# Attention, dense layer and routed experts on one core: three scheduling numbers moved

## The chip, the cores and the metric

The kernel runs on one core of one Trainium2 chip. The core's engines are TensorE (PE in the profile, with its weight loads as PEld), VectorE (DVE), ScalarE (ACT), GpSimd (POOL) and SyncE (SP), each working through its own instructions in order, and DMA queues that are fed by SP and POOL. The metric is the device time of one execution in microseconds; lower is better. Times are medians of several runs.

## What is computed

Three stages follow each other on 3072 tokens of width 384. First a gated linear attention over 4 sequences of 768 tokens with 8 heads of 48; then a dense layer 384 to 2048 to 384 with a leaky relu; then a layer of 8 experts to which the tokens are given greedily by their gate logits, 384 tokens to each.

```
for t in range(S):                                   # attention
    state = f[:, :, t, :, None] * state + np.einsum('bhd,bhe->bhde', k[:, :, t], v[:, :, t])
    y[:, :, t] = np.einsum('bhd,bhde->bhe', q[:, :, t], state)
...
h = x @ w_in                                         # dense layer
x = maximum(0.01 * h, h) @ w_out
...
logits = x @ w_gate                                  # routing: best pair first
for idx in argsort(-logits.flatten()):
    tok, e = idx // E, idx % E
    if assigned[tok] >= 0 or counts[e] >= N // E: continue
    assigned[tok] = e; counts[e] += 1
for e in range(E):                                   # experts
    h = maximum(x[assigned == e] @ w1[e], 0.0)
    out[assigned == e] = h @ w2[e]
```

## The kernel before

**Tiles.** The tokens are cut into 24 tiles of 128, taken chunk by chunk: tile n is chunk n // 4 of sequence n % 4. Precision is kept by splitting a number into a high and a low half of 16 bits, so a product takes three matmuls. The wide matmul of the kernel has 128 rows of weights and 384 columns; there are 3456 of them, in the dense layer (tiles `hp` and `xp`) and in the experts (`hp` from `x2T`, and `yp`).

**Attention of a tile.** `s0` sums logarithms of the forget gate (PSUM tile `P`), `s1` makes decayed queries and keys `qs` and `ks`, `s3` the scores `A`, `s2` transposes the keys on PE into PSUM (`kT`) and copies them on ACT to SBUF (`kp`), and `s4` makes the output `y` and the update `U` of the state, for which it reads `kp`. `attention()` walks over the tiles and gives one part, then yields a number of nanoseconds (`pace()`, 2300 once the dense layer runs), then the next part: `kT` in the third part of a tile and `y` and `U` one pace behind it. Tiles below FT = 8 are written out in another order at the start.

**Beside it.** The wide matmuls of the dense layer are the main stream. `Driver` advances a clock by the time of each wide matmul and puts the next part of a side generator into the program when its yield has run out; so a yield of 2300.0 stands for some 14 wide matmuls. The tile framework then sets the final order of each engine by its own priorities, unless `tc.keep_in_program_order` holds an instruction where it was written. Weights of the experts are loaded (`xw_s`), split on ACT (`xw_h`) and DVE (`xw_l`) and stored beside the dense layer. `gate_columns()` turns the rows of the second dense weight by a DMA transpose on SP's queue (`turned`) and multiplies them with the gate (`pg`, 12 small matmuls, 16 times); GP is the yield between the issue of a transpose and the matmuls of the one before it.

**Routing.** `route()` runs 7 rounds beside the last part of the dense layer and the first experts. A round looks for a threshold in 7 steps. Each step compares on DVE (`ge`), counts on PE (`c4`, six small matmuls), picks on DVE (`cm`, `cd`), sums on PE (`cnt`), compares on DVE (`ok`) and sums on PE (`tot`). At its end `slots_of` makes sums over tokens on PE (`ps`), and DVE works from them (`totc`, `inc`, `s1`) to the state of the next round, whose first step needs `ge` of some 29 DVE instructions later. The yield ahead of the first `c4` of a round is GAP[4] = 3400. For each finished round `token_list()` makes the list of tokens: DVE rows `ohs`, `h12`, `rh`, then PE `pi`, DVE, PE `pj`, DVE `idx` and `row`.

**Experts.** `fetch_weights` loads the weights of expert r (`w1e`, `w2e`) with POOL's queue; `fetch_tokens` gathers its tokens on POOL's queue (`xg`, three gathers) and turns them on SP's queue (`x2T<-xg`, three transposes). POOL also makes four of the eight `hl` halves of experts 1 to 5 and issues the scattered stores (`out`). All of them stand in one row on POOL. `w1e` of expert 7 waits until the three transposes of expert 6 have landed.

Every engine instruction goes through one helper, so the profile gives line 85 for all; rows are told apart by the names of their tiles. The profile drops trailing digits of names, so `c4` is `c`, `s1` is `s`, `x48` and `x2` are `x`.

Of the kernel before, what the change touches and what calls it, by code (L numbers as in the profile page):

```python
# [92 lines left out]
def body(tc, qk, v, f_logit, w_in, w_out, w_gate, w1, w2, out):  # L93
# [8 lines left out]
    E = w_gate.shape[1]  # L102
    NT = B * S // 128
# [7 lines left out]
    LEAD, PACE0, W0, FT, PB = 3, 1300.0, 1000.0, 8, 3  # L111

    with ExitStack() as ctx:
# [16 lines left out]
        def mm(o, l, r, start, stop):  # L130
            return PE.matmul(o, l, r, start=start, stop=stop, skip_group_check=True)
# [192 lines left out]
        XW = 768  # L324
        xw_s, xw_o = [], []
        assert SW1 == SW2
        PX, GP = 21, 3000.0

        turned_at = []
        fed, big = [], [0]  # L330
# [382 lines left out]
        def small(shape, name, dt=F32, bufs=2):  # L713
            return rw.tile(shape, dt, name=name, bufs=bufs)
# [6 lines left out]
        def route():  # L721
# [6 lines left out]
            for rnd in range(E - 1):  # L728
# [15 lines left out]
                oh = small([128, E, NT], "oh", BF16)  # L744
                DVE.tensor_tensor(oh, wdx, am[:, None, :].to_broadcast([128, E, NT]), op=OP.is_equal)
                DVE.scalar_tensor_tensor(v, d0, 1.0, un, op0=OP.add, op1=OP.mult)
                for l, (sh, w, T) in enumerate(LEVELS):
                    G = 128 // T
                    ge = small([128, NT * 32], "ge", BF16)[:, :NT * T].rearrange("p (a t g) -> p a t g", t=T, g=G)
                    va = v.rearrange("p (a g) -> p a g", g=G)[:, :, None, :].to_broadcast([128, NT // G, T, G])  # L750
                    DVE.tensor_tensor(ge, va, R["thr"][l], op=OP.is_ge)
                    if l == 0:
                        di = small([128, len(LEVELS) - 1, NT], "di", I32)
                        DVE.tensor_tensor(di, key[:, None, :].to_broadcast([128, len(LEVELS) - 1, NT]), R["sh"], op=OP.logical_shift_right)
                        DVE.tensor_tensor(di, di, R["mk"], op=OP.bitwise_and)
                        dg = small([128, len(LEVELS) - 1, NT], "dg", BF16)
                        DVE.scalar_tensor_tensor(dg, di, 1.0, R["unit"], op0=OP.add, op1=OP.mult)
                    yield GAP[0] if l else GAP[4]
                    c4 = bank([128, E, G], "c4")
                    for a in range(NT // G):  # L760
                        mm(c4, ge[:, a], oh[:, :, a * G:(a + 1) * G], a == 0, a == NT // G - 1)
                    wt = T.bit_length() - 1
                    cm = small([128, E * 8], "cm", F16)[:, :E * G].rearrange("p (e g) -> p e g", g=G)
                    DVE.tensor_tensor(cm, c4, R[f"diag{wt}"], op=OP.mult)
                    cd = R[f"cd{l % 2}"]
                    with nc.allow_low_precision("one count and zeros"):
                        DVE.tensor_reduce(cd[:, :E], cm, axis=AX.X, op=OP.add)
                    yield GAP[1]
                    cnt = bank([128, 32], "cnt")
                    mm(cnt[:, :T], cd, R[f"sel{wt}"], True, True)  # L770
                    ok = small([128, 32], "ok", BF16)
                    DVE.tensor_scalar(ok[:, :T], cnt[:, :T], kcap, None, op0=OP.is_ge)
                    yield GAP[2]
                    tot = bank([128, 32], "tot")
                    mm(tot[:, :T], R["bits"], ok[:, :T], True, True)
                    J = small([128, 1], "J")
                    scr = small([128, 32], "scr")
                    DVE.tensor_scalar(scr[:, :T], tot[:, :T], STEP[l], None, op0=OP.min, op1=OP.add, accum_out=J)
                    if l + 1 < len(LEVELS):
                        vp = v  # L780
                        v = small([128, NT], "v", BF16, 3)
                        DVE.scalar_tensor_tensor(v, vp, J, dg[:, l, :], op0=OP.subtract, op1=OP.add)
# [69 lines left out]
        GAP = (1700.0, 700.0, 550.0, 2000.0, 3400.0)  # L852
# [20 lines left out]
        def token_list(r, s):  # L873

            si = small([128, NT], "si", I32)
            DVE.tensor_scalar(si, s, -1.0, None, op0=OP.add)
            lo = small([128, NT], "lo", I32)
            DVE.tensor_scalar(lo, si, 31, None, op0=OP.bitwise_and)
            hi = small([128, NT], "hi", I32)
            DVE.tensor_scalar(hi, si, 5, None, op0=OP.arith_shift_right)  # L880
            lob = small([128, NT], "lob", BF16)
            DVE.tensor_scalar(lob, lo, 1.0, None, op0=OP.add)
            hib = small([128, NT], "hib", BF16)
            DVE.tensor_copy(hib, hi)
            yield 2500.0 if r else 600.0

            G = 4
            one = rw.tile([128, NT // G, 32, G], BF16, name="ohs", bufs=1)
            for h in range(2):
                x = slice(NT // G // 2 * h, NT // G // 2 * (h + 1))  # L890
                lg4 = lob.rearrange("p (a g) -> p a g", g=G)[:, x, None, :].to_broadcast([128, NT // G // 2, 32, G])
                DVE.tensor_tensor(one[:, x], lg4, R["thr5"][:, x], op=OP.is_equal)
                yield 300.0
            h12 = small([128, 12, NT], "h12", BF16)
            DVE.tensor_tensor(h12, hib[:, None, :].to_broadcast([128, 12, NT]), R["i12"], op=OP.is_equal)
            rh = small([128, 2, 12, NT], "rh", BF16)
            DVE.tensor_tensor(rh[:, 0], h12, R["jn"], op=OP.mult)
            DVE.tensor_scalar(rh[:, 1], h12, pcol, None, op0=OP.mult)
            yield 1500.0 if r == E - 2 else 1800.0
            pi = bank([128, 24, G], "pi")  # L900
            for a in range(NT // G):
                mm(pi, one[:, a], rh[:, :, :, a * G:(a + 1) * G].rearrange("p v h g -> p (v h) g"),
                   a == 0, a == NT // G - 1)
            pm = small([128, 24, G], "pm", F16)
            DVE.tensor_tensor(pm, pi, R["d15"][:, None, :].to_broadcast([128, 24, G]), op=OP.mult)
            pd = small([128, 24], "pd", F16)
            with nc.allow_low_precision("one whole number and zeros"):
                DVE.tensor_reduce(pd, pm, axis=AX.X, op=OP.add)
            yield 1200.0
            pj = bank([128, 6, 4], "pj")  # L910
            mm(pj, R["join"], pd, True, True)
            pq = small([128, 6, 4], "pq")
            DVE.tensor_tensor(pq, pj, R["quarter"][:, None, :].to_broadcast([128, 6, 4]), op=OP.mult)
            ti = small([128, 2, 3], "ti")
            DVE.tensor_reduce(ti.rearrange("p a b -> p (a b)"), pq, axis=AX.X, op=OP.add)
            idx = rw.tile([128, 3], I32, name="idx", bufs=E)
            DVE.scalar_tensor_tensor(idx, ti[:, 0, :], 128.0, ti[:, 1, :], op0=OP.mult, op1=OP.add)

            row = rw.tile([128, 3], I32, name="row", bufs=E)
            if r:  # L920
                DVE.tensor_scalar(row, idx, 1.0, None, op0=OP.add)
            else:
                f = small([128, 3], "f3")
                DVE.tensor_scalar(f, idx, 1.0, None, op0=OP.add)
                DVE.scalar_tensor_tensor(row, f, float(NT * 128 - 128), f, op0=OP.is_le, op1=OP.mult)
                DVE.tensor_scalar(R["place"], R["i384"], s[:, NT - 1:NT], None, op0=OP.is_equal)
            LISTS["x", r] = row, idx
# [147 lines left out]
        n = 0  # L1075
# [8 lines left out]
        def pace():  # L1084
            return 2300.0 if started else 1300.0
# [69 lines left out]
        def attention():  # L1155

            def finish(n):
                if (n < 0) or ("x", n) in complete:
                    return
                g, m = where[n]  # L1160
                if m == 0:
                    while g > 1 + done[0]:
                        yield 1000.0
                go("x", n)

            for n in range(NT):
                if ("x", n) in complete:
                    loads_after(n)
                    continue
                go("f", n + 1)  # L1170
                go("f", n + 2)
                go("p", n)
                go("a", n)
                yield pace()
                yield from finish(n - 1)
                go("p", n + 1)
                go("v", n)
                go("v", n + 1)
                yield pace()
                go("k", n)  # L1180
                yield pace()
                go("y", n)
                loads_after(n)
                yield pace()
            yield from finish(NT - 1)
# [156 lines left out]
```

## Time and profile before

| what | value |
|---|---|
| time, median of 3 runs | 754.88 us (753.85 to 755.87) |
| profiled execution, its own time | 762.14 us |
| its span, first to last instruction | 760.4 us |
| PE busy | 724.9 us, 95% of the span |
| DVE, ACT, POOL busy | 546.9, 338.8, 90.6 us |
| granted TensorE clock, mean | 0.990 |

PE is the engine to look at; the others are idle for a good part of the span. The profiled execution took 7.3 us more than the median. Busy time of PE is a union of matmuls that overlap: two wide matmuls in a row start 0.16 us apart, and each one's record lasts 0.33 us. The table of waits lists for each engine what it stood idle for, by the tile of the instruction that waited and the instruction that released it. The timeline gives start, length, engine, operation and tiles, with the idle time ahead and its releaser in brackets.

### The profile page before, as it was taken

The page shows a single profiled execution, that of the slowest core. Times are in us where ns is not written, and L with a number is a line of the kernel's source. Part 1 is how long each engine was busy: PE and PEld are TensorE (multiplying, and loading weights), DVE is VectorE, ACT ScalarE, POOL GpSimd, SP SyncE. Part 2 cuts the span into 40 slices and gives each one's busy share as a digit, 9 for nine tenths or more (in the row PEclk, how much of TensorE's full clock was granted, in tenths as well). Part 3 has the DMA queues.
Part 4 walks back from the last instruction along what each step waited for, and adds up shares of the span by engine and source line. Part 5 has one row for each costly group of instructions (what it writes and reads, how often), then busy time and mean ns, then how long its engine had stood idle before and what let it go on. Part 6 is the DMA issues. An engine that isn't in the chain of part 4 may idle for free.

```text
span 760.4 us, 15364 instructions
## 1 busy us (share of the span) xinstructions
PE 724.9 (95%) x5871; PEld 473.4 (62%) x5871; DVE 546.9 (72%) x1611; ACT 338.8 (45%) x704; POOL 90.6 (12%) x120
## 2 busy tenths in 40 slices
PE   8997999989999999999999999999999899999995
PEld 6774666667676677676666566555555455566563
DVE  7999999979857877876954758677686675863220
ACT  7677655557746755654744542000123123222220
POOL 3000000000000000000000001010234434534311
PEclk9998999999999999999999999999999999999998
DMA  9998555889896899998999200040475657664700
GB/s 235 216 235 218 141 155 137 205 242 256 225 290 172 263 273 220 250 278 215 238 254 247 94 2 13 22 187 22 155 223 164 189 151 180 215 173 142 252 32 32
DMA packets 116443, 137.08 MB, mean 180 GB/s; under 512 B 67729, under 2 KB 99474, under 8 KB 114322
## 3 DMA queue, kind: packets, MB, share of 16 engines
q1 hardware_dynamic: 110994, 101.50, 51.4%
q0 software_dynamic: 5376, 34.61, 13.4%
q8 instruction: 46, 0.75, 0.4%
q14 instruction: 27, 0.22, 0.1%
HBM read 86.52 MB, written 34.60 MB: 159 GB/s over the span
## 4 chain that ended last, share of the span: by engine, by line
PE 45%; DVE 25%; DMA 10%; issue 9%; ACT 4%; SPq 3%; POOL 2%; another core or an unknown queue 0%; POOLq 0%; ACTq 0%; DVEq 0%
PE xp L85 16%; PE hp L85 15%; PE yp L85 5%; DVE g L85 4%; DVE gl L85 3%; DMA xw_s<-in_moe_w 3%; PE y L85 3%; SPq L85 3%; DVE woutu L85 2%; DMA fT<-in_f_logit 2%; PE c L85 1%; ACT g L85 1%; PE A L85 1%; DVE am L85 1%; DVE xw_l L85 1%
## 5 line engine op out<-in xcount | busy, mean ns | idle before, releaser
L85 PE MATMUL hp<-xT,winh 128*128 128x384 f16 x768 | 192.2, 330 | 7.1 <-ACT winh L85 3.6
L85 PE MATMUL xp<-wo,gh 128*128 128x384 f16 x768 | 191.0, 326 | 1.0 <-ACT wo L85 1.0
L85 PE MATMUL hp<-xT,winl 128*128 128x384 f16 x384 | 126.6, 330 | 0.7 <-DVE winl L85 0.7
L85 PE MATMUL xp<-wo,gl 128*128 128x384 f16 x384 | 124.8, 325 | 0.0
L85 PEld LDWEIGHTS <-gh 128*128 128x128 f16 x912 | 83.6, 97 | 43.7 <-issue 1.2
L85 PEld LDWEIGHTS <-winh 128*128 128x128 f16 x768 | 73.6, 99 | 51.0 <-issue 6.1
L85 PE MATMUL hp<-x2T,w1e 128*128 128x384 f16 x576 | 99.0, 325 | 0.9 <-DVE x2T L85 0.5
L85 PE MATMUL yp<-w2e,hh 128*128 128x384 f16 x384 | 94.5, 325 | 0.0
L85 DVE SCALAR_TENSOR_TENSOR g<-hp,g 128x384 f32<-128x384 f32 x128 | 70.2, 554 | 26.1 <-ACT g L85 25.5
L85 ACT ACTIVATE g<-hp 128x384 f32<-128x384 f32 x148 | 70.0, 484 | 37.7 <-PE hp L85 25.8
L85 PEld LDWEIGHTS <-w1e 128*128 128x128 f16 x576 | 52.4, 97 | 33.8 <-issue 1.6
L85 ACT ACTIVATE xw_h<-xw_s 128x768 f16<-128x768 f32 x64 | 53.2, 840 | 30.4 <-DMA xw_s<-in_moe_w 24.5
L85 ACT ACTIVATE gh<-g 128x768 f16<-128x768 f32 x64 | 53.9, 842 | 28.5 <-DVE g L85 28.4
L85 PEld LDWEIGHTS <-gl 128*128 128x128 f16 x528 | 48.6, 97 | 28.8 <-issue 1.0
L85 DVE TENSOR_TENSOR gl<-g,gh 128x768 f16<-128x768 f32 x64 | 60.9, 952 | 2.3 <-ACT gh L85 2.3
L85 PE MATMUL yp<-w2e,hl 128*128 128x384 f16 x192 | 62.5, 325 | 0.0
L85 DVE SCALAR_TENSOR_TENSOR xw_l<-xw_s,xw_h 128x768 f16<-128x768 f32 x64 | 60.2, 952 | 1.2 <-ACT xw_h L85 1.1
L85 ACT ACTIVATE hh<-hp 128x384 f16<-128x384 f32 x64 | 31.3, 490 | 62.6 <-PE hp L85 50.2
L85 POOL IOTA jp<- 128x128 f32 x2 | 0.5, 237 | 454.7 <-PE hp L85 454.7
L85 DVE SCALAR_TENSOR_TENSOR hl<-hp,hh 128x384 f16<-128x384 f32 x44 | 24.3, 555 | 41.7 <-ACT hh L85 40.5
L85 PEld LDWEIGHTS <-winl 128*128 128x128 f16 x384 | 37.8, 99 | 24.9 <-DVE winl L85 2.0
L85 ACT ACTIVATE x<-yp 128x384 f32<-128x384 f32 x24 | 11.8, 490 | 92.2 <-PE yp L85 85.1
(262 smaller groups left out, 1116.5 us busy)
## 6 DMA issues: line engine op xcount, KB each, us to landing
xw_s<-in_moe_w SPq DMA_DIRECT2D x64, 384.0 KB, 4.1
qkT<-in_qk SPq DMA_DIRECT2D x48, 192.0 KB, 5.1
wout_s<-in_moe_w_out SPq DMA_DIRECT2D x16, 384.0 KB, 3.2
w1d<-xw_h SPq DMA_DIRECT2D x32, 192.0 KB, 3.3
w1d<-xw_l SPq DMA_DIRECT2D x32, 192.0 KB, 4.4
w2d<-xw_h SPq DMA_DIRECT2D x32, 192.0 KB, 3.7
w2d<-xw_l SPq DMA_DIRECT2D x32, 192.0 KB, 4.1
fT<-in_f_logit SPq DMA_DIRECT2D x24, 192.0 KB, 3.2
```

The costliest lines, as they stand in the source:

```text
L85: i = f(*args, **kwargs)
```

## The change

Three things are moved; nothing is added or removed. For tiles from FT on, `kT` is recorded one pace earlier, so two paces ahead of `y` and `U`. GP goes from 3000 to 4200. In rounds 1 to 3 the yield ahead of the first `c4` goes from 3400 to 5300 and these six matmuls are held in program order; and for the lists of rounds 1 and 2 the yield ahead of `pi` goes from 1800 to 3300.

```
-        PX, GP = 21, 3000.0
+        PX, GP = 21, 4200.0
...
-                    yield GAP[0] if l else GAP[4]
+                    yield GAP[0] if l else 5300.0 if 0 < rnd < 4 else GAP[4]
                     c4 = bank([128, E, G], "c4")
                     for a in range(NT // G):
-                        mm(c4, ge[:, a], oh[:, :, a * G:(a + 1) * G], a == 0, a == NT // G - 1)
+                        i = mm(c4, ge[:, a], oh[:, :, a * G:(a + 1) * G], a == 0, a == NT // G - 1)
+                        if l == 0 and 0 < rnd < 4:
+                            tc.keep_in_program_order(i)
...
-            yield 1500.0 if r == E - 2 else 1800.0
+            yield 1500.0 if r == E - 2 else 3300.0 if 0 < r < 3 else 1800.0
             pi = bank([128, 24, G], "pi")
...
                 go("v", n + 1)
+                if n >= FT:
+                    go("k", n)
                 yield pace()
-                go("k", n)
+                if n < FT:
+                    go("k", n)
                 yield pace()
                 go("y", n)
```

ACT, attention tile 13, the stretch ahead of its `ys<-y` (rows with - stand before, with + after):

```order
 L85 ACTIVATE xw_h<-xw_s 128x768
+L85 ACTIVATE kp<-kT 128x512
 L85 ACTIVATE gh<-g_2403 128x768
-L85 ACTIVATE xw_h<-xw_s 128x768
-L85 ACTIVATE kp<-kT 128x512
-L85 ACTIVATE xw_h<-xw_s 128x768
+L85 ACTIVATE xw_h<-xw_s 128x768 x2
 L85 ACTIVATE ys<-y 128x384
```

The copy `kp` moved ahead of `gh` and of one `xw_h`; on PE the four transposes `kT` of this tile moved from 15 to 30 wide matmuls ahead of `y`.

DVE, from the sums `ps` of round 2 on towards the `ge` of round 3 (`hl` belongs to expert 0), before:

```order
L85 COPY totc<-ps 128x48
L85 TENSOR_SCALAR wi<-mx,p_6230 128x1
L85 SCALAR_TENSOR_TENSOR hl<-hp,hh 128x384
L85 SCALAR_TENSOR_TENSOR inc<-ones,totc 128x48
L85 TENSOR_REDUCE m<-lg 128x24
L85 TENSOR_TENSOR inc<-inc,totc 128x48
L85 TENSOR_TENSOR eq_7640<-lg,m 128x192
L85 TENSOR_TENSOR s_7626<-ps,inc 128x48
L85 TENSOR_SCALAR key<-m 128x24
L85 TENSOR_TENSOR eq_7640<-eq_7640,wdt 128x192
L85 SCALAR_TENSOR_TENSOR hl<-hp,hh 128x384
L85 TENSOR_TENSOR s_7626<-s_7626,x_7590 128x48
```

The same stretch of DVE after:

```order
L85 COPY totc<-ps 128x48
L85 TENSOR_SCALAR wi<-mx,p_6230 128x1
L85 SCALAR_TENSOR_TENSOR inc<-ones,totc 128x48
L85 TENSOR_REDUCE m<-lg 128x24
L85 TENSOR_TENSOR inc<-inc,totc 128x48
L85 TENSOR_TENSOR eq_7673<-lg,m 128x192
L85 TENSOR_TENSOR s_7659<-ps,inc 128x48
L85 TENSOR_SCALAR key<-m 128x24
L85 TENSOR_TENSOR eq_7673<-eq_7673,wdt 128x192
L85 TENSOR_TENSOR s_7659<-s_7659,x_7621 128x48
```

The whole round has moved later beside the experts' stream, and three `hl` of expert 0 (a third one further down) no longer stand between `totc` and `ge`.

POOL, from the second `hl` of expert 5 to the weights of expert 7 (the first three `xg` are tokens of expert 6, the next three of expert 7), before:

```order
L85 TENSOR_TENSOR hl<-g_9699,hh 128x384
L85 DMA xg<-x2d,row 128x768
L85 TENSOR_TENSOR hl<-g_9766,hh 128x384
L85 DMA xg<-x2d,row 128x768 x2
L85 TENSOR_TENSOR hl<-g_9795,hh 128x384
L85 DMA w1e<-w1d,wi 128x6144
L85 DMA out<-x_9861,idx 3072x384
L85 DMA xg<-x2d,row 128x768 x3
```

The same stretch of POOL after:

```order
L85 TENSOR_TENSOR hl<-g_9669,hh 128x384
L85 TENSOR_TENSOR hl<-g_9717,hh 128x384
L85 TENSOR_TENSOR hl<-g_9751,hh 128x384
L85 DMA xg<-x2d,row 128x768 x3
L85 DMA out<-x_9834,idx 3072x384
L85 DMA w1e<-w1d,wi 128x6144
L85 DMA out<-x_9889,idx 3072x384
L85 DMA out<-x_9917,idx 3072x384
L85 DMA xg<-x2d,row 128x768 x3
```

The gathers for expert 6 moved behind all `hl` of expert 5 and stand together.

In numbers of wide matmuls on PE, from `ps` of the round ahead to the first `c4` of rounds 2 to 6: 29, 40, 32, 28, 26 before and 34, 33, 26, 26, 29 after. From `pj` of the list of expert r to the first matmul of expert r, for r = 4, 5, 6: 154, 135, 102 before and 117, 93, 66 after.

## Rows read from the trace of the kernel before

**Rows 1.** The page: its span, and PE's busy tenths in 40 slices.

```profile
span 760.4 us, 15364 instructions
...
PE   8997999989999999999999999999999899999995
```

**Rows 2.** Table of PE's waits: us in total, times, longest.

```profile
PE cnt L85 <- DVE cd L85: 3.6, 3, 2.2
...
PE c L85 <- DVE ge L85: 3.5, 7, 1.0
PE hp L85 <- DVE x L85: 2.1, 1, 2.1
...
PE U L85 <- ACT kp L85: 1.0, 3, 0.4
...
PE pi L85 <- DVE rh L85: 0.6, 1, 0.6
...
PE pg L85 <- DMA turned<-wo: 0.5, 1, 0.5
```

**Rows 3.** Timeline of ACT and PE at tiles 13 and 16.

```profile
198.99 0.84 ACT L85 ACTIVATE xw_h<-xw_s 128x768 f16<-128x768 f32 x1 [0.93 <-DMA xw_s<-in_moe_w]
199.74 0.58 ACT L85 ACTIVATE kp<-kT 128x512 f32<-128x512 f32 x1
...
200.37 0.83 PE L85 MATMUL U<-ld_v,kp 128*112 128x96 f32 x6 [0.35 <-ACT kp L85]
...
263.57 0.63 PE L85 MATMUL U<-ld_v,kp 128*112 128x96 f32 x4 [0.23 <-ACT kp L85]
```

**Rows 4.** Timeline of SP and PE at a gate column.

```profile
353.85 1.21 SPq L85 DMA_TRANSPOSE turned<-wo  x1
...
356.67 0.31 PE L85 MATMUL pg<-wgs,turned 128*128 128x16 f16 x6 [0.48 <-DMA turned<-wo]
```

**Rows 5.** Timeline of PE: first `c4` of rounds 2 to 5, and `ps` of round 2.

```profile
529.25 0.32 PE L85 MATMUL c<-oh,ge 128*128 128x32 bf16 x6 [0.40 <-DVE ge L85]
...
555.41 0.18 PE L85 MATMUL ps<-x,ones 128*128 128x48 bf16 x1
...
563.14 0.32 PE L85 MATMUL c<-oh,ge 128*128 128x32 bf16 x6 [1.02 <-DVE ge L85]
...
593.36 0.32 PE L85 MATMUL c<-oh,ge 128*128 128x32 bf16 x6 [0.81 <-DVE ge L85]
...
624.44 0.22 PE L85 MATMUL c<-oh,ge 128*128 128x32 bf16 x2 [0.35 <-DVE ge L85]
```

**Rows 6.** Timeline of DVE and POOL ahead of rounds 3 and 4.

```profile
555.12 0.23 DVE L85 TENSOR_SCALAR x<-asg,mx 128x24 bf16<-128x24 f32 x1
...
555.99 0.36 DVE L85 TENSOR_TENSOR lg<-lg,es 128x192 f32<-128x192 f32 x1
...
557.63 0.56 DVE L85 SCALAR_TENSOR_TENSOR hl<-hp,hh 128x384 f16<-128x384 f32 x1 [0.77 <-ACT hh L85]
...
562.52 0.56 DVE L85 TENSOR_TENSOR ge<-v,thr 128x768 bf16<-128x768 bf16 x1
...
587.15 0.91 POOL L85 TENSOR_TENSOR hl<-g,hh 128x384 f16<-128x384 f32 x1 [2.15 <-DVE x L85]
...
587.26 1.02 DVE L85 TENSOR_TENSOR lg<-lg,es 128x192 f32<-128x192 f32 x1
```

**Rows 7.** Timeline of PE and POOL for expert 6; view of `x2T`, its last line.

```profile
688.28 0.17 PE L85 MATMUL pj<-pd,join 128*128 128x24 f16 x1 [0.24 <-DVE pd L85]
...
701.08 0.96 POOL L85 DMA_INDIRECT w1e<-w1d,wi  x1 [5.87 <-DMA x2T<-xg]
...
705.00 0.65 PE L85 MATMUL hp<-x2T,w1e 128*128 128x384 f16 x3
...
DMA to landing us min/median/max: 2.7/3.4/9.8
```

**Rows 8.** Stretches of 20 us: busy time by engine, granted clock, DMA.

```profile
160.00:180.00 20.00, 18.59 (x149) 13.08 (x149) 17.52 (x33) 14.78 (x31) 0.00 (x0) 0.91 0.84 201
```

## The prediction

> **What bounds the kernel now.** The page comes first. PE is busy in nine tenths or more of nearly every slice of a span of 760.4 us [rows 1], so a change can only take back time in which PE stands still, and nothing here removes PE work. The second view is therefore the table of PE's waits, and the reader is to see how small its entries are [rows 2]: the longest groups are `cnt` behind `cd` with 3.6 us in 3 waits, `c` behind `ge` with 3.5 us in 7, one `hp` of 2.1 us, `U` behind `kp` with 1.0 us in 3, one `pg` of 0.5 us and one `pi` of 0.6 us. The change touches `kp`, `pg`, `c` and `pi`: 5.6 us in all, and not every one of these waits. Third, the timelines at those places tell what each wait is made of [rows 3 to 6].
>
> **What a wait costs.** Three wide matmuls in a row take 0.65 us, so one more costs 0.16 us, while a record lasts 0.33 us ([rows 7], the row at 705.00, and the front's table). After a wait this overlap has to build up again. I count each wait that goes, or comes, as its length plus 0.16 us.
>
> **Keys' transposes.** The instructions are the same; `kT` moves 15 wide matmuls or 2.5 us ahead on PE, and the copy `kp` moves ahead of one `xw_h` on ACT. At tile 13 one sees why this matters: `xw_h` waited 0.93 us for its load, `kp` stood behind it in ACT's row, started only as `xw_h` was over, and `U` waited 0.35 us for it [rows 3]. At tile 16 the same wait is 0.23 us. The third wait of this kind in the table is from the first tiles, which the change leaves alone. With 2.5 us of lead and one `xw_h` less in front, both waits go: 0.58 us and twice 0.16 us, **0.9 us gained**. `ks` is made a tile earlier, so `kT` waits for nothing new; it holds one of five PSUM buffers earlier by the same 2.5 us and gives it back earlier too. This I cost at nothing.
>
> **Gate columns.** 16 transposes and 16 groups of 12 small matmuls stay as they are; each group comes 1.2 us of stream later behind its transpose, and in the new order all 16 still stand ahead of the last dense group, which is the first to need them, so nothing is late at the end. One wait of 0.48 us ended with the landing of a transpose that SP had issued at 353.85, 2.8 us ahead of its group [rows 4]. That wait goes (0.64 us with the overlap). The transposes share three buffers with the outputs of the dense layer, and in the new order one transpose still gets its buffer only some 5.6 us of stream ahead of its group, about as the one that waited did; I leave 0.15 us for that: **0.5 us gained**.
>
> **First counts.** Per round the path is: `ps` on PE, 29 instructions on DVE, `c4` on PE. PE waits by what DVE takes more than the wide matmuls that stand in between. At round 3 DVE ran from 555.12 to 563.08 (`ge`, 562.52 and 0.56), 7.96 us, and PE filled 40 matmuls or 6.6 us from 555.41 on; the wait was 1.02 us [rows 5, 6]. Four `hl` stood in that chain; the order after shows one. The three that leave are worth 0.77 us of idle time ahead of the one at 557.63 and three times 0.47 us (0.56 us less the 0.09 us by which rows overlap), 2.2 us in all, so DVE needs 5.8 us [rows 6]. PE then has 33 matmuls, 5.4 us, and the small ones: a wait of about 0.1 us is left. Round 2: 34 matmuls instead of 29, 0.8 us more than enough for a wait of 0.40 us. Round 4 is not in the list of rounds that get a longer yield, and its count falls from 32 to 26 because its surroundings moved; its chain loses one `hl` (0.47 us) and the 0.66 us by which `lg` was longer there (1.02 against 0.36 us, [rows 6]), so 1.1 us less on DVE against 1.0 us less on PE: about 0.7 us left of 0.81. Round 5 loses two matmuls: 0.35 becomes 0.65 us. Round 6 gets 3 matmuls and one `hl` more and stays. The sum in us: 0.55 (round 2), 0.9 (round 3), 0.15 (round 4), less 0.3 (round 5), less 0.1 for `cnt` of round 3, which follows its `c4` one matmul closer: **1.2 us gained**.
>
> The row of `lg` at 587.26 lies on the `hl` that POOL ran from 587.15 to 588.06 [rows 6]. Round 6 moves onto the first `hl` of expert 4 and could be longer by the same 0.7 us; that is a bound, since only one of the DVE rows in the trace's round chains shows it. The Trainium skill (SBUF — State Buffer, section Who interferes with whom) says that a VectorE instruction with two inputs in SBUF and a GpSimd instruction that reads SBUF share a port which one of them holds to its end. The trace agrees: `lg` ended at 588.28, 0.2 us behind POOL. By that rule it is to be expected at round 6, and the gain here would be 0.5 us instead of 1.2.
>
> **Lists of rounds 1 and 2.** `pi` goes 1500 ns of stream later. The only wait of `pi` (0.6 us, [rows 2]) belongs to list 0, which is left as it is. So the gain is nothing; what it costs is in the next part.
>
> **What becomes late.** All routing from round 2 on moves down the PE row: at the end 36 wide matmuls, 5.9 us. Who is waiting there? Expert 6. Its list is done by `pj` at 688.28; `row`, three gathers and three transposes follow, and the last has landed as POOL's `w1e` of expert 7 is let go, close to 700.8 (5.87 us idle before 701.08) [rows 7]. That is 12.5 us, and expert 6 started at 705.00, 16.7 us after `pj`: a slack of 4.2 us. After, 66 matmuls or 10.8 us stand between instead of 102. If the 12.5 us stay, expert 6 waits 1.7 us. But the three gathers now stand together on POOL, without an `hl` of 0.91 us [rows 6] in between, so 11.6 us are nearer, and some 0.4 us of small matmuls lie in the gap: I take **0.4 us lost**, with bounds of 0 and 1.9.
>
> Expert 5 has 93 matmuls, 15.3 us, and some 2 us of small ones; against 12.5 us this is enough, at 0. Its upper bound: `w1e` of expert 6 now stands right behind its gathers, and a transpose has taken up to 9.8 us to land, against a median of 3.4 [rows 7]. 6.4 us more would make 18.9 us against 17.3: 1.6 us lost.
>
> **The sum.** 0.9 + 0.5 + 1.2 - 0.4 = 2.2 us. The profiled execution took 762.14 us and the median is 754.88; I carry the difference over: 754.88 - 2.2 = **752.7 us**. Bounds of this case: all gains and no loss at expert 6, 2.6 us and 0.3 that I held back, 752.0; with round 6 worse by 0.7 us, 753.4.
>
> **Rivals.**
>
> *The waits on transfers are not there without the profile.* The profiled execution is 7.3 us longer than the median, and the waits of `kp` and `pg` each end in a late load or transpose [rows 3, 4]. If loads are on time in other executions, 1.4 us of the gain were never lost. What stays is 1.2 - 0.4 = 0.8 us: 754.1 us. For it: the 0.93 us that `xw_h` waited. Against it: DVE's chain ahead of `c4` has no transfer in it.
>
> *The later routing starves the last experts: slower than before.* Place: the first matmuls of experts 5 and 6. Price: both upper bounds, 1.6 + 1.9 = 3.5 us, and by what the gain of transfers is missing: 754.88 - 1.2 + 3.5 = 757.2 us. It decides from the point where the two stalls together exceed the gain, 1.2 to 2.6 us. For it: one transpose in the trace did take 9.8 us. Against it: the list's own chain got shorter on POOL. The Trainium skill (DMA: Bandwidth & Descriptors, section Queues, rings and completion order) says that the DMA engines take turns between queue rows packet by packet, by which a small transpose would not stand behind a whole block of weights; the landing of 9.8 us speaks against that here, and by the rule the price would be 1.9 us, 755.6 us.
>
> *A larger stall dissolves.* The `hp` wait of 2.1 us [rows 2] at 161 us ends behind DVE's `x`, which ACT's row had held up; in that stretch PE was at a granted clock of 0.91, so for a part of it at the lower of its two levels, which costs 9% of 20 us [rows 8]. `kp` moves ahead in ACT's row in the tiles before. If that undoes it, 2.3 + 1.8 us come on top: 748.6 us, or about half of this, 750.6. Against it: ACT's wait there was for a load, not for `kT`.
>
> *The change does not do what it says.* The order shows the moves on PE, ACT and POOL, so this is only left as the first rival.
>
> **How the numbers follow.** Forecast 0.50, transfers on time 0.22, starved experts 0.14, larger stall gone 0.14. What a measurement of this kernel can tell from no change is about 0.3%, 2.3 us: faster is below 752.6, slower above 757.1. The forecast lies on that line: half of it, 0.25, counts as faster; with 0.14 of the larger stall and little of the rest, faster 0.40. Slower: of the starved experts 0.10. The same: 0.50. Range: from half of the larger stall, 750.4, to within the starved case, 756.6; outside are the full dissolution and the worst of the starved case, 0.07 and 0.08.
>
> **What would show it.** In the profile after: no `U` behind `kp` from tile 8 on; no `pg` wait of 0.5 us behind `turned<-wo`; `c` behind `ge` near 0 at rounds 2 and 3, near 0.7 at rounds 4 and 5; a first `hp` of expert 6 that waits up to about 1 us for a transpose. Wrong would be: those waits gone and the time unchanged; a wait of 2 us and more at expert 5 or 6; or a new wait of `ps` or `cd` in rounds 1 to 3.

## The result and the profile after

| what | before | after |
|---|---|---|
| median of 7 runs | 754.88 us (752.73 to 756.17) | 760.78 us (757.99 to 763.41) |
| ratio, 95% interval | 1 | 1.0077 (1.0058 to 1.0096) |
| profiled execution, its own time | 762.14 us | 760.90 us |
| DVE busy in the profile | 546.9 us | 554.9 us |

The change made the kernel slower by 0.77%, 5.9 us, where 2.2 us were forecast as a gain. Three more comparisons of the same two kernels gave 1.0044, 1.0087 and 1.0071.

The two profiles hide this: the profiled execution of after is the shorter one. That of before held four delays: the `hp` wait of 2.1 us at 161 us and the 1.8 us of lower clock behind it [rows 2, 8], and two `cnt` waits of 1.2 and 2.2 us at 574 and 606 us [rows 2]. They sum to 7.3 us, as much as this execution took above the median. None of them is in the profile after, and the attention part alone has none either. That they are the whole difference is argued and not shown: there is one profile of before, and `cnt` waits of 1.1 to 1.3 us stand in the profiles of experiments 6, 9, 10 and 11 too. What is compared here are the waits beyond these four.

The page of after, its span, its busy times and PE's tenths in 40 slices:

```profile
span 759.1 us, 15368 instructions
...
PE 722.1 (95%) x5871; PEld 472.9 (62%) x5871; DVE 554.9 (73%) x1611; ACT 337.3 (44%) x704; POOL 90.5 (12%) x120
...
PE   8997899999999999999999999999999999898995
```

The loss stands at the right end: slices 35 and 37, which were at 9, are at 8 [rows 1], and DVE is busy for 8 us more with the same 1611 instructions. The table of PE's waits after (us in total, times, longest):

```profile
PE c L85 <- DVE ge L85: 3.8, 6, 2.2
PE hp L85 <- DMA x2T<-xg: 2.6, 2, 1.4
PE ps L85 <- DVE x L85: 1.6, 2, 1.4
...
PE pj L85 <- DVE pd L85: 0.8, 2, 0.6
...
PE cnt L85 <- DVE cd L85: 0.5, 1, 0.5
...
PE U L85 <- ACT kp L85: 0.4, 1, 0.4
```

Against [rows 2], `U` behind `kp` is left only in the first tiles (at 23 us), `pg` behind `turned<-wo` is gone, and `c` behind `ge` has about the same sum, 3.8 us against 3.5, with one long wait in it. New are `hp` behind `x2T` and `ps`. The timeline of PE after, from 640 us on, the rows that waited for DVE or a transfer:

```profile
653.91 0.32 PE L85 MATMUL c<-oh,ge 128*128 128x32 bf16 x6 [2.21 <-DVE ge L85]
676.03 0.81 PE L85 MATMUL hp<-x2T,w1e 128*128 128x384 f16 x4 [1.38 <-DMA x2T<-xg]
679.87 0.18 PE L85 MATMUL ps<-x,ones 128*128 128x48 bf16 x1 [0.22 <-DVE x L85]
684.69 0.18 PE L85 MATMUL ps<-x,ones 128*128 128x48 bf16 x1 [1.36 <-DVE x L85]
691.97 0.17 PE L85 MATMUL pj<-pd,join 128*128 128x24 f16 x1 [0.59 <-DVE pd L85]
704.27 0.97 PE L85 MATMUL hp<-x2T,w1e 128*128 128x384 f16 x5 [1.27 <-DMA x2T<-xg]
```

That is the first count of round 6, expert 5, the sums of round 6, the last sums, a list and expert 6: 7.0 us of waits. In the profile of before the same stretch has two, 0.24 us of `pj` at 688.28 [rows 7] and the first count of round 6:

```profile
653.84 0.32 PE L85 MATMUL c<-oh,ge 128*128 128x32 bf16 x6 [0.45 <-DVE ge L85]
```

What holds DVE up is seen ahead of the first count of round 6, in DVE's and POOL's timelines of after:

```profile
648.85 1.00 POOL L85 DMA_INDIRECT w1e<-w1d,wi  x1 [0.30 <-issue]
649.36 1.57 DVE L85 TENSOR_TENSOR eq<-eq,wdt 128x192 bf16<-128x192 bf16 x1
649.87 0.92 POOL L85 TENSOR_TENSOR hl<-g,hh 128x384 f16<-128x384 f32 x1
...
652.08 0.54 DVE L85 SCALAR_TENSOR_TENSOR hl<-hp,hh 128x384 f16<-128x384 f32 x1
652.21 0.91 POOL L85 TENSOR_TENSOR hl<-g,hh 128x384 f16<-128x384 f32 x1 [1.41 <-ACT g L85]
652.55 0.78 DVE L85 TENSOR_TENSOR oh<-wdx,am__9170 128x192 bf16<-128x192 bf16 x1
```

`eq` takes 1.57 us and ends at 650.93, 0.14 us behind POOL's `hl`; `oh` takes 0.78 us and ends 0.2 us behind the next. Without POOL's `hl` beside them they take 0.25 and 0.35 us (experiment 1, below). With one DVE `hl` more (0.47 us net) DVE's chain is 1.32 + 0.43 + 0.47 = 2.2 us longer. PE had waited 0.45 us here and now has three wide matmuls, 0.5 us, more to fill the time with, so a wait of about 2.2 us is what this comes to, and what was measured. `eq` began 0.5 us ahead of POOL's `hl`, beside the issue of `w1e`; what held it in that half microsecond is not shown. From 560 us on, 16 DVE rows of the profile after are over 0.1 us longer than their kind and lie beside a POOL row, 15 of them beside an `hl`: they are 10.4 us longer together. In the profile of before there are 6, 4 of them beside an `hl`, and 2.5 us.

Why they meet can be counted in the program. An expert is 144 wide matmuls, in the first 72 `hp` is made and with it the `hl`, in the second 72 there are none. The second halves of experts 1 to 4 are the wide matmuls 2520 to 2592, 2664 to 2736, 2808 to 2880 and 2952 to 3024. The sums `ps` of a round open DVE's long chain to the first count of the next round, those of round 6 the chain to the last sums. Before, the sums of rounds 3 to 6 stood at 2517, 2681, 2845 and 3009, so the chains to the first counts of rounds 4 to 6 ran almost wholly inside a second half. After, they stand at 2553, 2717, 2881 and 3045: the chain to the first count of round 6 and the last sums have slid into the first half of the next expert.

### The profile page after: what moved, and what is told of

It reads as the page before. It is cut to its first block, busy times and chain, and to the rows that moved or that the text cites. A ratio compares the mean times of both kernels' runs of the same rounds, so it can differ in the third digit from the quotient of the medians.

```text
span 759.1 us, 15368 instructions
## 1 busy us (share of the span) xinstructions
PE 722.1 (95%) x5871; PEld 472.9 (62%) x5871; DVE 554.9 (73%) x1611; ACT 337.3 (44%) x704; POOL 90.5 (12%) x120
## 4 chain that ended last, share of the span: by engine, by line
PE 53%; DVE 23%; DMA 10%; issue 7%; ACT 4%; POOL 2%; SPq 1%; POOLq 0%; ACTq 0%; DVEq 0%
PE hp L85 20%; PE xp L85 18%; PE y L85 4%; PE yp L85 4%; DVE g L85 3%; DMA fT<-in_f_logit 2%; DVE gl L85 2%; DMA x2T<-xg 2%; DVE woutu L85 2%; PE A L85 2%; DMA xg<-x2d,row 2%; PE U L85 1%; DMA xw_s<-in_moe_w 1%; PE P L85 1%; PE c L85 1%
## 5 line engine op out<-in xcount | busy, mean ns | idle before, releaser
L85 PE MATMUL hp<-xT,winh 128*128 128x384 f16 x768 | 190.0, 327 | 8.0 <-ACT winh L85 5.4
L85 PEld LDWEIGHTS <-hh 128*128 128x128 f16 x384 | 36.3, 97 | 22.4 <-issue 0.8
```

Source lines behind the costliest of these rows:

```text
L85: i = f(*args, **kwargs)
```

## Experiments

Each ratio is to the kernel before on the same chip in the same runs, with its 95% interval.

### The two halves of the change, and lateness alone

Experiment 1 keeps the attention part (`kT` and GP), experiment 2 the routing part (yields, pin, lists), word for word as in the change. Experiment 3 only delays:

```
-                    yield GAP[0] if l else GAP[4]
+                    yield GAP[0] if l else 3400.0 + 6000.0 if rnd == 1 else GAP[4]
```

> Only the keys' transposes (one pace earlier) and GP 4200; the routing is as before. Theory L (late routing): what the change lost sits in the last experts, where the profile of after shows 2.2 us at the first c4 of round 6, 1.4 at expert 5, 1.4 at ps of the last sums, 0.6 at a pj and 1.3 at expert 6, 7 us together; then this kernel has none of it and keeps the small gains of the dense stage: 753.5 us, 0.5 to 1.5 us under before, and no U behind kp from tile 8 on. Theory D (dense stage): the moved transposes cost something that a profile hides, a share of the lower clock for instance; then this kernel takes 759 to 761 us. Theory U (untypical profile): the waits that the change took away were not there in the timed executions; then it takes 754.9 us, equal to before within 0.3%.

> Only the routing part: first counts of rounds 1 to 3 with 5300 and in program order, lists of rounds 1 and 2 with 3300; dense stage as before. Theory L: all of the loss, 760.5 to 762.5 us, with the waits of after at round 6, expert 5, the last sums and expert 6. Theory D: no loss, 753.7 us, since 1.2 us of waits at rounds 2 to 4 go. Theory U: between, 755 to 758 us, the rest of the loss from both parts together.

> The kernel before with one number more: ahead of the first c4 of round 1 alone the yield is 9400 instead of 3400. From round 4 on the sums ps stand within one wide matmul of where they stand after (2554, 2718, 2882, 3046 wide matmuls against 2553, 2717, 2881, 3045), but nothing else of the change is there. Theory L (lateness alone does it): 760 to 763 us with the same waits at round 6, experts 5 and 6 and the last sums. Theory R (not lateness, but the order that the longer yields and the pinned counts make inside rounds 1 to 3 and their lists): 755 to 757 us, with waits at rounds 2 and 3 instead.

Measured: 0.9964 (0.9949 to 0.9979), 1.0115 (1.0098 to 1.0132) and 1.0110 (1.0093 to 1.0128). So the attention part is a gain of 0.36%, 2.7 us, and the routing part a loss of 8.7 us; together a loss of 6.0, against 5.9 in the result. A delay without anything else of the change costs the same as the routing part. PE's waits of experiment 2 and of experiment 3:

```profile
PE c L85 <- DVE ge L85: 3.8, 6, 2.2
PE hp L85 <- DMA x2T<-xg: 2.1, 2, 1.1
...
PE ps L85 <- DVE x L85: 1.4, 2, 1.1
```

```profile
PE c L85 <- DVE ge L85: 4.8, 7, 2.2
PE ps L85 <- DVE x L85: 1.5, 2, 1.2
PE hp L85 <- DMA x2T<-xg: 1.3, 1, 1.3
```

Experiment 1 has neither `x2T` nor `ps` in its table, and its chain of round 6 runs at its usual pace (DVE and PE):

```profile
638.50 0.25 DVE L85 TENSOR_TENSOR eq<-eq,wdt 128x192 bf16<-128x192 bf16 x1
...
639.94 0.35 DVE L85 TENSOR_TENSOR oh<-wdx,am__9124 128x192 bf16<-128x192 bf16 x1
...
640.82 0.32 PE L85 MATMUL c<-oh,ge 128*128 128x32 bf16 x6 [0.45 <-DVE ge L85]
```

### Keys alone

Experiment 9 moves `kT` only; GP stays at 3000.

> Only the keys' transposes one pace earlier; GP, the routing and the lists as before. The kernel with this and GP 4200 was 0.36% under before (2.7 us), where the prediction had 0.9 us for the keys and 0.5 us for the gate columns. If the keys carry it in these proportions: 1.7 us under before, no U behind kp from tile 8 on and the pg wait of 0.5 us behind turned<-wo still there. If the gate columns carry it: within 0.7 us of before.

Measured: 0.9983 (0.9967 to 1.0000), 1.3 us. No `U` waited behind `kp` from tile 8 on, and without GP the columns still wait, here longer than in the profile of before:

```profile
PE pg L85 <- DMA turned<-wo: 1.8, 2, 1.4
PE U L85 <- ACT kp L85: 0.4, 1, 0.4
```

By these values about half of the 2.7 us is from the keys and the rest from GP. The interval of experiment 9 reaches from no gain to 2.5 us and overlaps that of experiment 1, so this split is not shown.

### Taking POOL's `hl` away

In the changed kernel (5) and in the attention part alone (6), the eight `hl` of experts 4 and 5 that POOL made go to DVE:

```
-                    if f % 2 == 0 and 0 < r < E - 2:
+                    if f % 2 == 0 and 0 < r < 4:
```

> The changed kernel, with the four hl of experts 4 and 5 that POOL made moved to DVE, so that from expert 4 on POOL reads no tiles for arithmetic. Theory K (collisions): in the profile of after a DVE row that starts beside a POOL hl ends only with it, 16 rows and 10 us against 6 rows and 2.5 us before, because the later routing has moved its chains of DVE rows from the second half of an expert, where no hl stand, into the first half, where they do. Of the 10 us, 6 lie from 649 us on, and go here; eight hl of 0.47 us come onto DVE instead. By K c4 of round 6 waits 1 us instead of 2.2, the last sums 0.3 to 0.9 instead of 1.4, a pj 0.1 instead of 0.6, and expert 6 0 to 0.5 instead of 1.3: 3 to 4 us less than the changed kernel in the same runs. Theory L (lateness as such): the lists are as late as before in wide matmuls (pj of expert 5 even 12 later), so experts 5 and 6 wait as they did: within 1 us of the changed kernel, or slower.

> The control for the run before: the same eight hl moved to DVE in the kernel with the attention part and gate columns alone, where the chains of rounds 5 and 6 stand in the second half of an expert. Theory K: only three of its long DVE rows lie there, 1.4 us and none ahead of a waiting c4; no gain, 0 to 0.7 us slower than that kernel (749.9 us at a before of 753.1). If moving hl to DVE is good whatever the place of the rounds, it gains 1 us or more.

> The changed kernel again, for comparison on the same chip: 0.6 to 1.0% above before, and again c4 of round 6 behind ge with 2.2 us, the last sums with 1.4 us, and DVE rows of the routing that last until a POOL hl ends.

Measured on one chip: 1.0003 (0.9990 to 1.0015) for 5, 0.9969 (0.9954 to 0.9984) for 6, 1.0044 (1.0023 to 1.0065) for the changed kernel. Moving the `hl` gives the changed kernel 0.41%, 3.1 us, though DVE has more to do; where the chains stand in second halves it gives nothing (0.9969 against 0.9964 of experiment 1, on another chip). In the profile of 5, DVE's rows and the first count of round 6, then the waits:

```profile
651.88 0.25 DVE L85 TENSOR_TENSOR eq<-eq,wdt 128x192 bf16<-128x192 bf16 x1
...
653.53 0.35 DVE L85 TENSOR_TENSOR oh<-wdx,am__9170 128x192 bf16<-128x192 bf16 x1
...
654.41 0.32 PE L85 MATMUL c<-oh,ge 128*128 128x32 bf16 x6 [0.32 <-DVE ge L85]
```

```profile
PE tot L85 <- DVE ok L85: 3.8, 3, 2.1
...
PE hp L85 <- DMA x2T<-xg: 1.7, 1, 1.7
PE c L85 <- DVE ge L85: 1.7, 5, 0.5
...
PE ps L85 <- DVE x L85: 0.2, 1, 0.2
```

2.2 us at round 6 became 0.3, the last sums lost their wait, expert 5 does not wait, and expert 6 still does, 1.7 us. I had expected 0 to 0.5 there; its list is still late. The `tot` waits have another source: 2.1 us of them stand behind a standstill of DVE at 571 us (last section) and 1.3 us, at 670 us, behind another 1.7 us in which DVE did nothing.

The edit also takes eight rows each from ACT and POOL, and the stall of expert 5 went with it, so this pair alone does not show that the whole gain is collisions. Experiments 13 and 14 below help: expert 5 waits in neither, they ran on one chip, and they differ by this edit alone, 1.0052 against 1.0013, which is 0.39%, 2.9 us. So POOL's `hl` beside the late chains is shown as a cause, for about 3 us.

### Half a step instead of a whole one

The attention part, and of the routing only this:

```
-                    yield GAP[0] if l else GAP[4]
+                    yield GAP[0] if l else 3900.0 if 0 < rnd < 4 else GAP[4]
```

The sums stand 9 wide matmuls later from round 3 on, at 2526, 2690, 2854 and 3018.

> The attention part and gate columns, and the yield of the first c4 of rounds 1 to 3 at 3900 instead of 3400, no pin and the lists as before: from round 4 on the sums stand 9 wide matmuls later than before, not 36. Theory K: the chain of round 4, which began at the end of an expert's first half (2517 against 2520 wide matmuls) and met a POOL hl (lg 1.02 us), moves wholly into the second half: its c4 waits 0.3 instead of 0.8 us; round 6 ends at 2880, just where the next first half starts, and keeps 0.45; the last sums move onto the first hl of expert 5 and could lose 0.5: within 0.7 us of the kernel with the attention part alone. Theory L: a quarter of the loss of the full shift (8.1 us), so 2 us slower than that kernel.

> The kernel with the attention part, gate columns at 4200 and the small shift (3900 in rounds 1 to 3), again: it was 0.46% under before. By theory K its chains of rounds 4 and 5 stand in the second halves of experts, and it is 0.3 to 0.5% under before again; on this chip it is also 6 us or more under the changed kernel.

Measured: 0.9954 (0.9938 to 0.9971) and 0.9977 (0.9967 to 0.9988). It is faster than before on both chips, and level with the attention part (0.9964 and, in 6, 0.9969). A quarter of the shift costs nothing that these runs can tell, so the loss is not in proportion to the lateness. The chain of round 4 lost its meeting: `lg` takes 0.36 us instead of 1.02 [rows 6], and its first count waits 0.49 us instead of 0.81 [rows 5], in the first run:

```profile
580.99 0.36 DVE L85 TENSOR_TENSOR lg<-lg,es 128x192 f32<-128x192 f32 x1
...
585.98 0.32 PE L85 MATMUL c<-oh,ge 128*128 128x32 bf16 x6 [0.49 <-DVE ge L85]
```

The sums of round 3 took that gain back: they waited 0.49 us at the end of a chain of DVE rows in which `abv`, 0.97 us instead of 0.23, had met an `hl`.

### Tokens that are ready: inconclusive

Experiments 4, 11 and 12 let experts 5, 6 and 7 take the list of expert 4 (their own tokens are left out), 12 with the `hl` of experts 4 and 5 on DVE:

```
-            xg = gather(LISTS["x", r][0], x2d)
+            xg = gather(LISTS["x", min(r, 4)][0], x2d)
```

> The changed kernel, but experts 5, 6 and 7 take the tokens of the list of expert 4, which is made long before, so these experts no longer wait for a late list (left out: their own tokens; the number of gathers, transposes and matmuls is the same). Theory L says that the stalls of experts 5 and 6 (1.4 and 1.3 us and 0.16 us each) are due to late lists: about 3 us less than the changed kernel, 757.8 us; what stays over before then sits at round 6, the last sums and a pj (4 us). If the two stalls come from the transposes' queue whatever their list, the time stays at 760 to 761 us.

> The changed kernel with experts 5, 6 and 7 taking the tokens of the list of expert 4 (left out: their own tokens), now beside the changed kernel on one chip. Theory L + K (both late lists and collisions cost): the stalls of experts 5 and 6 go, 2.7 to 4.2 us in the profiles of the changed kernel, and some 1.5 us come at counts that meet the earlier gathers of POOL, as the profile of the earlier run showed (1.1 us at 636 us, 0.5 us more at round 6): 1 to 3 us less than the changed kernel. If the experts' stalls only stand in for other waits, the time is the same within 0.7 us.

> The changed kernel with both taken away: experts 5, 6 and 7 take the tokens of the list of expert 4 (left out: their own tokens), and the hl of experts 4 and 5 are all made by DVE. If late lists and collisions together are the loss, this comes to where the kernel with the attention part and gate columns alone stood, 0.3 to 0.4% under before, 6 to 8 us less than the changed kernel; if a third cause is in the later routing, it stays above before.

> The changed kernel once more, as the reference for the two kernels that follow on this chip: 0.4 to 0.8% above before; c4 of round 6 waits 2.2 us, the last sums 1.4 us, experts 5 and 6 wait 1 to 3 us each.

Measured: 1.0069 (1.0054 to 1.0083) for 4; then on one chip 1.0087 (1.0060 to 1.0113) for 11, 1.0062 (1.0038 to 1.0086) for 12 and 1.0087 (1.0064 to 1.0110) for the changed kernel. The stalls of experts 5 and 6 went, and the time did not: nine of POOL's gathers now stood beside the routing, from 632 to 645 us in 11, and PE waited there instead (11: `cnt` 6.5 us in 4 waits). The longest of these, 4.1 us, is a standstill of DVE that the last section shows; whether the gathers caused it is not shown. The edit moved more than it took away, so it says nothing on what the late lists cost.

### The weights behind the tokens

What experiments 4 and 11 could not tell, this one tells for expert 5: `w1e` of expert 6 waits on POOL until the transposes of expert 5 have landed, in the changed kernel (13) and together with the `hl` on DVE (14).

```
-            ... or (r == E - 1 and r - 1 not in turned_x):
+            ... or (r >= E - 2 and r - 1 not in turned_x):
...
+                elif r == E - 2 and n == 0:
+                    for x in turned_x[r - 1]:
+                        after(i, x)
```

> The changed kernel, with the weights w1e of expert 6 held on POOL until the three transposes of expert 5 have landed, as the kernel does for expert 7 already. In the profiles of the changed kernel these weights were issued 0.8 us ahead of the second transpose, which then took 9.9 us to land, and expert 5 started 1.2 to 2.7 us late. If the weights in front are the cause, the second transpose lands in 3 to 4 us, expert 5 does not wait, and the time is 1.3 to 2.7 us less than the changed kernel in the same runs. If the transposes are slow for another reason, the second still takes 9 us and more, and POOL, held up, makes it worse: 0 to 2 us more.

> The changed kernel with both: w1e of expert 6 behind the transposes of expert 5, and the hl of experts 4 and 5 on DVE. The run with hl on DVE alone stood level with before (1.0003), and expert 6 waited 1.7 us in it, while expert 5 just did not wait. So the weights' place should add little here, 0 to 1 us: 0.1% under before to level with it. What is left over the kernel with the attention part alone (0.35% under before, 2.7 us) would be the 1.7 us of expert 6 and the rest of the later routing.

> The changed kernel again, as the reference for these two on one chip: 0.4 to 0.9% above before.

Measured on one chip: 1.0052 (1.0037 to 1.0068) for 13, 1.0013 (1.0001 to 1.0025) for 14, 1.0071 (1.0057 to 1.0085) for the changed kernel. In the profile after, SP issued the second transpose of expert 5 at 664.93, 0.8 us behind POOL's `w1e`, and it landed at 674.83, 9.9 us later (POOL and SP, the view of `x2T` at this transpose, and SP's next row):

```profile
664.11 0.95 POOL L85 DMA_INDIRECT w1e<-w1d,wi  x1 [0.31 <-issue]
...
664.93 1.21 SPq L85 DMA_TRANSPOSE x2T<-xg  x1
...
DMA to landing us min/median/max: 9.9/9.9/9.9
...
666.28 4.08 SPq L85 DMA_TRANSPOSE x2T<-xg  x1
```

PE went on at 676.03, 1.2 us behind this landing. Its wait ended with the third transpose, issued at 666.28, which took 4.1 us on SP instead of 1.2 and whose landing the profile does not list.

In 13 the second transpose, issued at 661.58, landed at 664.52, 2.9 us later, the third took its 1.2 us on SP, and expert 5 does not wait; only expert 6 is left (SP, the view of `x2T` at this transpose, and POOL, then PE's waits):

```profile
661.58 1.21 SPq L85 DMA_TRANSPOSE x2T<-xg  x1
...
DMA to landing us min/median/max: 2.9/2.9/2.9
...
667.45 0.95 POOL L85 DMA_INDIRECT w1e<-w1d,wi  x1 [6.69 <-DMA x2T<-xg]
```

```profile
PE hp L85 <- DMA x2T<-xg: 1.0, 1, 1.0
```

So the profiles show the weights in front as the cause of expert 5's stall. What it is worth in the time is 0.19%, 1.4 us, but the two intervals overlap, so it is not shown to be a gain. Both remedies together take 0.58%, 4.4 us. 14 stays 0.36%, 2.7 us, above the small shift on the same chip (0.9977), and its profile has 1.6 us at expert 6, which no run took away alone; the last 1.1 us I could not place.

```profile
PE hp L85 <- DMA x2T<-xg: 1.6, 1, 1.6
```

## Why the prediction was wrong

**The keys, right, and too small.** No `U` waited behind `kp` from tile 8 on. With GP the attention part gave 2.7 us (1.6 to 3.8) for the 1.4 that I had summed. By the first rival, in which the waits on transfers are not there without the profile, it would have gained nothing; the table of experiment 9 shows that `pg` can wait for longer than the 0.48 us that I read.

**Gate columns, right.** The wait behind `turned<-wo` is gone.

**First counts, rounds 2 to 5, right.** I had 0 for round 2, 0.1 for round 3, 0.7 and 0.65 for rounds 4 and 5; after has none, none, 0.50 and 0.46 us (timeline of PE after, rounds 4 and 5):

```profile
591.24 0.32 PE L85 MATMUL c<-oh,ge 128*128 128x32 bf16 x6 [0.50 <-DVE ge L85]
...
621.20 0.32 PE L85 MATMUL c<-oh,ge 128*128 128x32 bf16 x6 [0.46 <-DVE ge L85]
```

**Round 6, mis-sized.** I wrote that it "stays", at 0.45 us, with 0.7 more as a bound, from the one `lg` that the trace showed next to an `hl`. It became 2.2. I had seen that the chain moves onto "the first `hl` of expert 4", but it is over 6 us long and two of POOL's lie in it, and one of the two rows was 1.3 us longer, twice the price that I had read. The Trainium skill (SBUF — State Buffer, section Who interferes with whom) says that the shared port is an exclusive lock for the whole instruction. The trace agrees: `eq` ended 0.14 us behind POOL, and DVE's `hl` at 652.08, which has one input in PSUM, took its usual 0.54 us beside POOL's.

**What becomes late: the step that failed.** The sum has 0.4 us lost for it; the routing part, with its gains at the first counts, lost 8.7 us. I asked of the 5.9 us only who waits for a list, and found the experts. I did not ask beside what the whole second part of the routing would now run. The sums of round 6 and the last sums (1.6 us), a list (0.6), `tot` (0.4) stand in no term. The price was in the trace: the `hl` at 587.15 and the row of `lg` [rows 6], and the order gave the places. In its place the runs showed some 3 us of time for DVE rows held beside POOL's `hl`, 1.4 us, not clear of the noise, for the weights ahead of expert 5's transposes, and a last 2.7 us, of which 1.6 stand at expert 6 in a profile; the cause of the other 1.1 stays open.

**Expert 6, mis-sized within its bounds.** I took 0.4 us and named 1.7 if the 12.5 us from `pj` to the last landing stay. They nearly stayed: 691.97 to 704.13 is 12.2 us, and the wait was 1.3, in experiment 5 1.7. Three gathers in a row brought the tokens 0.3 us nearer, where I had put 0.9.

**Expert 5, mis-sized.** It was costed at 0 with 1.6 as the upper bound, for the reason that then held: the profile after has 1.4 us, and another of the same kernel (experiment 8) 2.7. The Trainium skill (DMA: Bandwidth & Descriptors, section Queues, rings and completion order) has the engines take turns between queue rows; read as I did, it leaves nothing of this stall. The landing of 9.9 us, and of 2.9 with the weights behind, speaks against that reading for this transfer.

**The rivals.** Starved experts had the right sign and a 0.14. Its price, 3.5 us, was for two experts alone; the routing part lost 8.7. The larger stall is not in the profile after, but it was one of the four delays of that one execution, and the median of after did not fall.

**The difference of 7.3 us**, carried over unread, was harmless for the sum. Tracing it to those four delays would have hinted at what the typical execution holds.

## What to carry to other kernels

When a change slides one stream along another, lay both out in the same unit and see beside what each long chain now runs; do so before asking who waits for its result. An engine that is 12% busy can be the costly neighbour if its instructions shut another out for their whole length. A bound that a row in the trace has already shown once is a term of the sum with a chance, and not 0.

## What the hardware showed

**One-input rows are held too.** On the way to list 6, DVE's `lo` and `hib` of one input took 0.92 and 0.89 us, elsewhere 0.16 to 0.18, beside POOL's `hl` (POOL's and DVE's timelines of after):

```profile
686.54 0.92 POOL L85 TENSOR_TENSOR hl<-g,hh 128x384 f16<-128x384 f32 x1 [3.58 <-ACT g L85]
686.57 0.92 DVE L85 TENSOR_SCALAR lo<-si 128x24 int32<-128x24 int32 x1
...
689.47 0.93 POOL L85 TENSOR_TENSOR hl<-g,hh 128x384 f16<-128x384 f32 x1 [2.01 <-ACT g L85]
689.54 0.89 DVE L85 CAST hib<-hi 128x24 bf16<-128x24 int32 x1
```

**DVE stood still for nothing that the trace names.** In experiment 11, `cm` waited 4.81 us although its count had long ended, and PE stood for 4.1 us behind it; in the ten microseconds after, the granted clock was 0.83, for a part of them at the lower of its two levels (DVE's timeline, the transfers of an instruction queue from 648 to 649 us, and the stretch with the clock, the 0.83):

```profile
649.43 0.23 DVE L85 TENSOR_TENSOR cm<-c,diag 128x64 f16<-128x64 f32 x1 [4.81 <-remote]
...
q14 instruction: 1, 0.01, 1.9%
...
650.00:660.00 10.00, 9.39 (x50) 5.09 (x50) 7.93 (x52) 2.73 (x6) 3.01 (x4) 0.83 0.25 77
```

A packet of an instruction queue moved within the last 1.5 us ahead of the restart; in experiment 12 it was the same near 650 us. The page of 11 counts 73 such packets in 763 us, one in some 10 us, so both can lie there by chance. The Trainium skill (Runtime: NRT & Kernel Launch, section Instruction fetch mechanics) says that engines fetch their code ahead and that this is mostly hidden. Stalls of this kind, 2.5 to 3.4 us, are in the profile of before at 606 us and in those of experiments 5, 10, 11 and 12 near 570 us, and no instruction packet shows beside these. So the cause stays open; such a stall comes in some executions of a kernel and not in others.
